# Earlier weight chunks, spread first sums and rearranged ends in a thresholded attention and squared-ReLU FFN kernel

## The chip, the core and the metric

The kernel runs on one core of a Trainium2 chip. The core has five engines that run side by side and wait for each other through semaphores: TensorE (PE; its weight loads are listed as PEld), VectorE (DVE), ScalarE (ACT), GpSimd (POOL) and SyncE (SP), which here only issues DMA transfers. Matrix products go to PSUM, everything else lies in SBUF, and large tensors lie in HBM. The metric is the device time of one execution in microseconds, from the first to the last instruction.

## What is computed

The reference, cut to what matters:

```python
# q, k, v: (8, 8, 576, 64) float32; tau = 0.02; w_in (512, 2048), w_out (2048, 512)
scores = q @ k.T / 8
scores = where(scores >= max(scores) - tau, scores, -1e9)
attn = exp(scores - max(scores)); attn = attn / (sum(attn) + 1e-9)
x = (attn @ v), as (4608, 512)           # batch and sequence x heads and head size
h = maximum(x @ w_in, 0.0)
out = (h * h) @ w_out                    # (4608, 512)
```

The two weight matrices arrive as float64, since their scaling in numpy made them so; the kernel turns them into float32 itself.

## The kernel before

**Attention.** Two heads make a pair, and there are 32 pairs (`pairs`, line 265). Each pair's 576 query rows are cut into five blocks (four of 128, one of 64 for both heads), so there are 160 blocks (`slots`, line 482). `slot(n)` (line 556) is an order written out by hand: in program order it names, for each engine, what is done for block n and its neighbours. Scores are computed three blocks ahead (`ahead(n + 3, ...)`), the softmax follows in steps (`stage`, `second`: maximum on DVE, exponential on ACT, threshold and sum on DVE, reciprocal on DVE at line 387, normalising on GpSimd at line 396), the weights are transposed on TensorE (line 437) and copied out of PSUM by ACT (line 439), and the product with v (line 467) gives a block of x^T, which is stored to HBM (`give_x`, `ask`). Score tiles (`sc`) have two PSUM buffers and so have all other PSUM tiles of this stage (`b`).

`load(i)` (line 268) asks for q and k of a pair: for each of the two, two transfers for the first 512 rows of both heads and one for the remaining 64 rows. All requests go out on the SP queue in program order, and a request whose buffer isn't free holds up those behind it. `turn(i)` transposes q and k, and `turn_last(i, ...)` does the remaining rows; after that the next pair is asked for.

**Weights.** Between these steps the weights are converted. There are 32 chunks of 512 KB as they arrive (16 of w_out, then 16 of w_in; `chunks`, line 161). `starts` (line 530) gives the block at which each begins: every second block from 0 for w_out, and every second block from `IN_FIRST` = 76 for w_in. With the chunk that begins at block s, `fetch` is called in block s - 1 and asks for it on the SP queue, into one of three buffers `raw`; `convert1` (ACT, line 201) and `convert2` (ACT) are in block s + 1, `convert3` (GpSimd) in s + 2, `convert4` and `convert5` (DVE) in s + 3, and `convert6` (GpSimd, line 239) in s + 4 makes the float32 chunk and frees the buffer.

**Sums.** The FFN multiplies 2x2 blocks of blocks with seven products in place of eight, on two levels, so that 49 products of sums are made. `sums` makes the sums of the weights on GpSimd, one per block by `sums_step`: those of w_out from block 35 on (`OUT_SUMS`, 44 of them), those of w_in from block 111 on (`IN_SUMS`). The first 512 tokens' sums of x^T (`prepare_x(0, ...)`, 12 of them) are made on GpSimd inside the attention: `load_x(0)` after block 24, and one sum after each block from 26 on (lines 885 to 889).

**FFN.** The tokens go through in nine steps of 512. `hidden_layer(n, also)` makes squared hidden values and stores them to HBM; when all steps are done, `output_layer(n, also)` makes the output. In each, a loop over seven outer products (`OUTER`) runs `inner`, with seven inner ones of four matmuls each; `inner` hands four finished quarters of an outer product to `final`. In the output layer, `final` adds into `t3` on DVE, and after `inner` one instruction on GpSimd (`sums_to(slice(1, 4), nc.gpsimd, ...)`, line 855) adds three of the four quarters to the running sums U2, U3 and to the output tile `o`. After the outer products 5 and 3, which end a half of the output rows, four stores are put in the list `later`; `ask()` issues them on the SP queue, at a later tick or, for the last half of the last step, after everything (line 983).

**The ends.** The program begins with building the identity matrix, asking for tau (line 110), `load(0)`, `load_v(0)`, the transposes of the first pair, and three blocks from -3 on that only start scores.

Of the kernel before, what the change touches and what calls it, by code (L numbers as in the profile page):

```python
# [11 lines left out]
I32 = mybir.dt.int32  # L12
# [36 lines left out]
def kernel(  # L49
# [25 lines left out]
    nc = tc.nc  # L75
    B, H, S, D = q.shape
    P = 128
# [8 lines left out]
    MAIN = FULL * P  # L86
    STEP = 512
    NSTEP = B * S // STEP
# [15 lines left out]
    sb = Region(arena, 0, X_AT[0])  # L104
# [2 lines left out]
    make_identity(nc, ident)  # L107

    tau_c = const.tile([P, 1], FP32, name="tau_c")
    nc.sync.dma_start(  # L110
        out=tau_c[:, :], in_=bass.AP(tensor=tau.tensor, offset=tau.offset, ap=[[0, P], [1, 1]])
    )

# [18 lines left out]
    def plus(e, out, x, y):  # L132
        e.tensor_tensor(out=out, in0=x, in1=y, op=ALU.add)  # L133
# [26 lines left out]
    WC = 512  # L160
# [11 lines left out]
    def fetch(m):  # L172
        if m is None:
            return
        src = chunks[m][3]
        three = (lambda t: t.rearrange("p (k o) -> p k o", k=4)) if m < 16 else (lambda t: t)
        if src.dtype == FP32:
            nc.sync.dma_start(out=three(weight(m)[:, :]), in_=src)
            return
        raw = sb.tile([P, 2 * WC], I32, tag="raw", bufs=3, name="raw")  # L180
        nc.sync.dma_start(out=three(raw[:, :]), in_=src.bitcast(I32))
        raws[m] = raw

# [78 lines left out]
    later = deque()  # L262
# [5 lines left out]
    def load(i):  # L268
        b, hp = pairs[i]
        h = 2 * hp  # L270
        qn = sb.tile([P, FULL, P], FP32, tag="qn", name="qn")
        kn = sb.tile([P, FULL, P], FP32, tag="kn", name="kn")

        rn = sb.tile([P, P], FP32, tag="rn", name="rn")

        for src, dst, order, rows in ((q, qn, "(t p) d -> p t d", 0), (k, kn, "(p t) d -> p t d", REST)):
            for j in range(2):
                nc.sync.dma_start(out=dst[:, :, ds(j * D, D)], in_=src[b, h + j, 0:MAIN, :].rearrange(order, p=P))
            nc.sync.dma_start(
                out=rn[ds(rows, REST), :].rearrange("p (j d) -> p j d", j=2),  # L280
                in_=src[b, h : h + 2, MAIN:S, :].rearrange("j p d -> p j d"),
            )
        loaded[i] = (qn, kn, rn)

    def load_v(i):
        b, hp = pairs[i]
        h = 2 * hp
        va = sb.tile([P, 2, FULL, D], FP32, tag="va", bufs=2, name="va")
        vd = vdiag[i % 2]
        nc.sync.dma_start(out=va[:, :, :, :], in_=v[b, h : h + 2, 0:MAIN, :].rearrange("j (p t) d -> p j t d", p=P))  # L290
        for j in range(2):
            nc.sync.dma_start(out=vd[ds(j * D, D), ds(j * D, D)], in_=v[b, h + j, MAIN:S, :])
        loaded_v[i] = (va, vd)

    def turn(i):

        qn, kn, rn = loaded.pop(i)
        qT = sb.tile([P, S], FP32, tag="qT", bufs=2, name="qT")
        kT = sb.tile([P, S], FP32, tag="kT", bufs=2, name="kT")
        turning[i] = (qT, kT, rn)  # L300
        for nat, to in ((qn, qT), (kn, kT)):
            pt = bank([P, FULL, P], "pqk")
            for t in range(FULL):
                nc.tensor.transpose(pt[:, t, :], nat[:, t, :], ident[:, :])
            flat, to = pt[:, :, :].rearrange("p t m -> p (t m)"), to[:, 0:MAIN]
            if nat is kn:
                nc.scalar.copy(to, flat)  # L307
            else:
                nc.scalar.activation(out=to, in_=flat, func=AF.Identity, scale=qscale[:, :])
            yield  # L310
# [242 lines left out]
    def begun(n):  # L553
        return starts.get(n)

    def slot(n):

        sums_start(n)
        ask()
        turn_part(n - 1, "w")  # L560
        convert4(begun(n - 3))
        convert3(begun(n - 2))
        stage(n + 2)
        turn_step(n, 0)
        values_and_load(n - 2)
        convert1(begun(n - 1))
        stage(n + 1)
        second(n + 1)
        turn_part(n - 1, "R")
        second(n + 2)  # L570
        sums_step()
        turn_part(n - 1, "W")
        convert6(begun(n - 4))
        stage(n + 2)
        second(n + 2)
        fetch(begun(n + 1))
        convert5(begun(n - 3))
        ahead(n + 3, 0)
        stage(n + 1)
        turn_step(n, 1)  # L580
        ahead(n + 3, 1)
        convert2(begun(n - 1))
# [229 lines left out]
    def output_layer(n, also):  # L812
        bank = lambda: banks.tile([P, BANK], FP32, tag="b", bufs=6, name="po")[:, 0:P]
        temp = lambda name: fin.tile([P, P], FP32, tag="t")
        AT = {(0, 0): 0, (1, 1): 1, (1, 0): 2, (0, 1): 3}
        U2 = fin.tile([P, 4, P], FP32, tag="u")
        U3 = fin.tile([P, 4, P], FP32, tag="u")
        o = {}
        for m in OUTER:
            where = {2: (0, 0), 4: (1, 0), 5: (1, 1), 3: (0, 1)}.get(m)  # L820
            if where and where[0] not in o:
                o[where[0]] = fin.tile([P, 2, 4, P], FP32, tag="o")
            mine = U3 if m in (4, 5) else U2
            t3 = fin.tile([P, 3, P], FP32, tag="t3") if m != 1 else None

            def product(to, k, more):
                g, w = operands[n, m, k], W_OUT[m, k].rearrange("p (k o) -> p k o", k=4)
                for j in range(4):
                    nc.tensor.matmul(  # L829
                        to, g[:, j, :], w[:, j, :], start=(not more and j == 0), stop=(j == 3), skip_group_check=True  # L830
                    )

            def sums_to(i, e, c):

                if where:
                    plus(e, o[where[0]][:, where[1], i, :], c, mine[:, i, :])
                if m in (5, 6):
                    plus(e, U2[:, i, :], c, U2[:, i, :])
                if m == 7:
                    plus(e, U3[:, i, :], c, U2[:, i, :])  # L840

            def final(ab, c, other):
                i = AT[ab]
                if m == 1 and other is None:
                    nc.scalar.copy(U2[:, i, :], c)
                elif m == 1:
                    plus(nc.vector, U2[:, i, :], c, other)
                elif other is None:
                    sums_to(i, nc.vector, c)
                else:  # L850
                    plus(nc.vector, t3[:, i - 1, :], c, other)

            inner(product, copy, temp, bank, final, lambda at: also(m, at))
            if m != 1:
                sums_to(slice(1, 4), nc.gpsimd, t3[:, :, :])
            if m in (5, 3):
                row = where[0]
                for (a, b), i in AT.items():
                    to = out[ds(n * STEP + row * 2 * NQ + a * NQ, NQ), :].rearrange("p (c b o) -> p c b o", c=2, b=2)
                    later.append((to[:, :, b, :], o[row][:, :, i, :]))  # L860


    def spread(work, at):
# [5 lines left out]
    with tc.manual_schedule():  # L869
        with ExitStack() as stack:  # L870
            sc_pool = stack.enter_context(tc.tile_pool(name="sc", bufs=2, space=PSUM))
            b_pool = stack.enter_context(tc.tile_pool(name="b", bufs=2, space=PSUM))

            def bank(shape, name):
                return b_pool.tile(shape, FP32, tag="b", name=name)

            load(0)
            load_v(0)
            for _ in turn(0):
                pass  # L880
            turn_last(0, bank([P, P], "pqkr")[:, :])()
            load_v(1)
            for n in range(-3, len(slots)):
                slot(n)
                if n == 24:
                    load_x(0)
                    xsums = prepare_x(0, lambda op, out, x, y: op(nc.gpsimd, out, x, y))
                if n > 25:
                    next(xsums, None)
            n = len(slots)  # L890

            def drain():

                while pending:
                    pt, m, of = pending.popleft()
                    xr = sb.tile([P, 2, P], FP32, tag="xr", bufs=3)
                    nc.scalar.copy(xr[:, 0, 0:m], pt[:, 0, 0:m])
                    give_x(of, xr)

            drain()  # L900
            values_and_load(n - 2)
            for part in "RWw":
                turn_part(n - 1, part)
            values_and_load(n - 1)
            drain()
            for _ in range(60):
                sums_step()
            ask()
# [111 lines left out]
```

## Time and profile before

| | |
|---|---|
| time, median of 3 | 1486.08 us (1485.96 to 1487.52) |
| span of the profiled execution | 1487.0 us, clock 0.994 |
| PE / DVE / ACT / POOL busy | 97% / 68% / 60% / 71% |
| attention, block 0 to its last copy (line 897) | 18.2 to 682.9 us |
| FFN, both layers | 682.9 to 1487.0 us |
| DMA, mean over the span | 119 GB/s |

A profile page gives for each engine its busy time, and the span in forty slices with the busy share of each in tenths. The list of waits says which engine sat idle in front of which line and what ended that: "ACT arena L201 <- DMA ..." is ScalarE idle before line 201 until a transfer landed. The chain of waits is followed back from the last instruction, and each of its pieces is the one that released the next. In the timeline a row has the start, the time, the engine, line and operation, and in brackets the idle time ahead of it. A row of busy time by stretch has the stretch, its length, the busy time of PE, PEld, DVE, ACT and POOL with the number of instructions, the granted TensorE clock, the busy share of the DMA engines and GB/s. An engine's mean busy share says little here, since the attention, the hidden layer and the output layer have different limits.

### The profile page before, as it was taken

The numbers are of one execution on the slowest core, as the hardware profiler recorded it, in microseconds if no ns is written. First come the engines' busy times: TensorE is split into PE (matmuls) and PEld (weight loads), VectorE is DVE, ScalarE is ACT, GpSimd is POOL, SyncE is SP. The second block draws the span as 40 slices with busy tenths as digits, with TensorE's granted clock in tenths as the row PEclk, the third lists the DMA queues.
The fourth block names the chain that finished last, engine by engine and source line by source line (L and its number), as shares of the span: only waits on it lengthen the run. The fifth ranks groups of instructions, "written<-read, shape, count | busy, mean of one in ns | idle before, by whom it ended". The sixth has DMA issues, their size and how long they took to land.

```text
span 1487.0 us, 35254 instructions
## 1 busy us (share of the span) xinstructions
PE 1437.3 (97%) x12880; PEld 1214.7 (82%) x12880; DVE 1006.9 (68%) x2149; ACT 888.9 (60%) x1792; POOL 1052.9 (71%) x1319
## 2 busy tenths in 40 slices
PE   6999999999999999999999999999999999999998
PEld 3665566665666666668999999999999999999998
DVE  4877766667777666775778877778755666555653
ACT  4887777767877777765666656767543333323330
POOL 3777987877767887773666555566677787777775
PEclk9999999999999999999999999999999999999999
DMA  4345223557343222212332334332994432244411
GB/s 110 104 118 156 61 54 97 166 175 218 100 117 106 64 63 56 58 40 67 121 126 95 114 114 143 135 122 100 368 333 143 143 111 82 98 139 143 143 29 29
DMA packets 212956, 176.90 MB, mean 119 GB/s; under 512 B 99888, under 2 KB 161328, under 8 KB 212784
## 3 DMA queue, kind: packets, MB, share of 16 engines
q1 hardware_dynamic: 212784, 174.65, 37.5%
q8 instruction: 102, 1.67, 0.5%
q14 instruction: 70, 0.57, 0.1%
HBM read 105.12 MB, written 69.47 MB: 117 GB/s over the span
## 4 chain that ended last, share of the span: by engine, by line
PE 61%; DVE 15%; ACT 8%; POOL 6%; DMA 5%; issue 3%; SPq 1%; POOLq 0%; DVEq 0%; ACTq 0%
PE po L829 27%; PE ph L706 21%; DVE arena L381 9%; ACT arena L376 5%; PE sc L353 5%; DVE arena L364 4%; PE pvR L467 3%; PE pwT L437 3%; PE sc L338 2%; POOL arena L396 1%; DVE arena L133 1%; DMA w<-w 1%; POOL w L130 1%; ACT arena L307 1%; POOL arena L133 1%
## 5 line engine op out<-in xcount | busy, mean ns | idle before, releaser
L133 POOL TENSOR_TENSOR arena<-arena 128x512 f32<-128x512 f32 (+1 forms) x315 | 377.5, 1221 | 258.5 <-DVE arena L133 220.7
L829 PE MATMUL po<-w,arena 128*128 128x128 f32 x3528 | 397.9, 276 | 2.1 <-ACT arena L620 1.8
L829 PEld LDWEIGHTS po<-w,arena 128*128 128x128 f32 x3528 | 396.3, 193 | 3.6 <-ACT arena L620 2.0
L706 PE MATMUL ph<-arena,w 128*128 128x128 f32 x3528 | 396.6, 275 | 2.1 <-DVE arena L133 1.1
L706 PEld LDWEIGHTS ph<-arena,w 128*128 128x128 f32 x3528 | 394.7, 192 | 3.9 <-DVE arena L133 3.5
L133 DVE TENSOR_TENSOR arena<-ph,arena 128x512 f32<-128x512 f32 x378 | 255.5, 688 | 93.9 <-PE ph L706 53.7
L364 DVE TENSOR_REDUCE arena<-sc 128x1 f32<-128x576 f32 x288 | 217.3, 755 | 131.6 <-PE sc L353 131.6
L381 DVE SCALAR_TENSOR_TENSOR arena<-sc,arena 128x576 f32<-128x576 f32 x288 | 224.5, 813 | 21.8 <-ACT arena L376 21.2
L396 POOL TENSOR_SCALAR arena<-arena 128x576 f32<-128x576 f32 (+1 forms) x320 | 223.0, 707 | 7.5 <-DVE arena L387 3.3
L133 DVE TENSOR_TENSOR arena<-po,arena 128x128 f32<-128x128 f32 x378 | 108.0, 289 | 172.1 <-PE po L829 169.2
L652 ACT COPY c<-arena 128x512 f32<-128x512 f32 (+1 forms) x303 | 172.7, 579 | 62.1 <-DVE arena L130 56.3
L376 ACT ACTIVATE arena<-sc,arena 128x576 f32<-128x576 f32 x288 | 200.7, 747 | 14.3 <-DVE arena L364 9.9
L437 PEld LDWEIGHTS pwT<-ident,arena 128*128 128x128 f32 x1152 | 128.6, 141 | 90.5 <-issue 36.2
L437 PE MATMUL pwT<-ident,arena 128*128 128x128 f32 x1152 | 181.5, 280 | 12.9 <-ACT arena L416 9.5
L353 PE MATMUL sc<-arena 64*128 64x512 f32 (+2 forms) x768 | 185.8, 575 | 1.3 <-DVE arena L381 1.0
L130 POOL TENSOR_TENSOR arena<-arena 128x512 f32<-128x512 f32 (+1 forms) x138 | 174.9, 1267 | 9.7
L130 DVE TENSOR_TENSOR arena<-arena,c 128x512 f32<-128x512 f32 (+1 forms) x267 | 174.5, 662 | 7.5 <-ACT c L652 6.9
L439 ACT COPY arena<-pwT 128x512 f32<-128x512 f32 x256 | 151.6, 592 | 46.1 <-PE pwT L437 36.3
L467 PE MATMUL pvR<-arena 128*64 128x128 f32 (+1 forms) x2560 | 164.2, 269 | 5.0 <-ACT arena L439 0.7
L467 PEld LDWEIGHTS pvR<-arena 128*64 128x64 f32 x2560 | 128.6, 137 | 34.9 <-issue 19.6
L685 ACT ACTIVATE arena<-arena 128x512 f32<-128x512 f32 x144 | 89.9, 624 | 77.6 <-POOL arena L133 77.6
L620 ACT COPY arena<-po 128x128 f32<-128x128 f32 x63 | 16.7, 265 | 180.5 <-PE po L829 178.5
(53 smaller groups left out, 1147.3 us busy)
## 6 DMA issues: line engine op xcount, KB each, us to landing
g<-arena SPq DMA_DIRECT2D x144, 256.0 KB, 2.0
arena<-g SPq DMA_DIRECT2D x144, 256.0 KB, 4.6
w<-w SPq DMA_DIRECT2D x98, 256.0 KB, 4.8
out_dram<-arena SPq DMA_DIRECT2D x72, 128.0 KB, 2.2
arena<-in_q_dram SPq DMA_DIRECT2D x64, 128.0 KB, 2.7
arena<-in_k_dram SPq DMA_DIRECT2D x64, 128.0 KB, 2.9
arena<-in_v_dram SPq DMA_DIRECT2D x32, 256.0 KB, 2.8
arena<-in_moe_w_out_dram SPq DMA_DIRECT2D x16, 512.0 KB, 4.2
```

The costliest lines, as they stand in the source:

```text
L130: e.tensor_tensor(out=out, in0=x, in1=y, op=ALU.subtract)
L133: e.tensor_tensor(out=out, in0=x, in1=y, op=ALU.add)
L353: nc.tensor.matmul(to, qT[rows, ds(t * P, m)], kT[rows, ds(k0, n)], start=True, stop=True)
L364: nc.vector.tensor_reduce(out=nmx[:, j : j + 1], in_=sc[:, ds(at[j], S)], axis=AXIS.X, op=ALU.max, negate=True)
L376: nc.scalar.activation(out=w[:, ts(j, S)], in_=sc[:, ds(at[j], S)], func=AF.Exp, bias=nmx[:, j : j + 1], scale=1.0)
L381: nc.vector.scalar_tensor_tensor(out=w[:, ts(j, S)], in0=sc[:, ds(at[j], S)], scalar=thr[:, j : j + 1], in1=w[:, ts(j, S)], op0=ALU.is_ge, ...
L396: nc.gpsimd.tensor_scalar(out=out, in0=w, scalar1=r, scalar2=1.0, op0=ALU.mult, op1=ALU.mult)
L437: nc.tensor.transpose(pt[:, c, :], w[:, ds(j * (S + REST) + c * P, P)], ident[:, :])
L467: nc.tensor.matmul(pv[rows, :], va[:, j, c, :], wT[:, j, c, 0:n], start=(c == 0), stop=False, skip_group_check=True)
L652: nc.scalar.copy(c, y)
L706: nc.tensor.matmul(to[:, j, :], W_IN[m, k][:, ts(j, P)], of[k][:, m - 1, :], start=(not more and j == 0), stop=True, skip_group_check=True,)
L829: nc.tensor.matmul(to, g[:, j, :], w[:, j, :], start=(not more and j == 0), stop=(j == 3), skip_group_check=True)
```

## The change

It has four parts. Weight chunks are asked for two blocks sooner, and four raw buffers take the place of three. The load and the sums of the first x^T are moved from blocks 24 to 37 to blocks 76 to 111, and one sum is made every third block instead of every block. At the start, tau and the first pair's k are asked for on the ACT queue instead of the SP queue, so that two sequencers issue at once, and TensorE gets transposes of the identity that nobody reads (ten at first, twelve after each of blocks -2 and -1), which are meant to bring its clock up. At the end, the last outer product of the last step makes its last sums on DVE, quarter by quarter, and stores each at once, in turn on the SP and the ACT queue, instead of one sum on GpSimd and stores after it.

```diff
-    nc.sync.dma_start(
+    nc.scalar.dma_start(
         out=tau_c[:, :], in_=bass.AP(tensor=tau.tensor, offset=tau.offset, ap=[[0, P], [1, 1]])
...
-        raw = sb.tile([P, 2 * WC], I32, tag="raw", bufs=3, name="raw")
+        raw = sb.tile([P, 2 * WC], I32, tag="raw", bufs=4, name="raw")
...
+            queue = nc.scalar if i == 0 and src is k else nc.sync
             for j in range(2):
-                nc.sync.dma_start(out=dst[:, :, ds(j * D, D)], in_=src[b, h + j, 0:MAIN, :].rearrange(order, p=P))
-            nc.sync.dma_start(
+                queue.dma_start(out=dst[:, :, ds(j * D, D)], in_=src[b, h + j, 0:MAIN, :].rearrange(order, p=P))
+            queue.dma_start(
...
-        fetch(begun(n + 1))
+        fetch(begun(n + 3))
...
+        def give_out(row, ab, queue):
+            a, b = ab
+            to = out[ds(n * STEP + row * 2 * NQ + a * NQ, NQ), :].rearrange("p (c b o) -> p c b o", c=2, b=2)
+            if queue is None:
+                later.append((to[:, :, b, :], o[row][:, :, AT[ab], :]))
+            else:
+                queue.dma_start(out=to[:, :, b, :], in_=o[row][:, :, AT[ab], :])
...
+            at_end = n == NSTEP - 1 and m == OUTER[-1]
...
                 else:
                     plus(nc.vector, t3[:, i - 1, :], c, other)
+                    if at_end:
+                        sums_to(i, nc.vector, t3[:, i - 1, :])
+                if at_end:
+                    give_out(0, ab, nc.sync if i % 2 else nc.scalar)
...
-            if m != 1:
+            if m != 1 and not at_end:
                 sums_to(slice(1, 4), nc.gpsimd, t3[:, :, :])
...
+            def keep_busy(times):
+                pt = bank([P, P], "idle")
+                for _ in range(times):
+                    nc.tensor.transpose(pt[:, :], ident[:, :], ident[:, :])
...
+            keep_busy(10)
             for _ in turn(0):
                 pass
...
                 slot(n)
-                if n == 24:
+                if -3 < n < 0:
+                    keep_busy(12)
+                if n == IN_FIRST:
                     load_x(0)
                     xsums = prepare_x(0, lambda op, out, x, y: op(nc.gpsimd, out, x, y))
-                if n > 25:
+                if n > IN_FIRST + 1 and n % 3 == 0:
                     next(xsums, None)
```

More of the change, by code (lines that the diff above doesn't have):

```diff
@@ L851, in final @@
                     plus(nc.vector, t3[:, i - 1, :], c, other)
+                    if at_end:
+                        sums_to(i, nc.vector, t3[:, i - 1, :])
+                if at_end:
+                    give_out(0, ab, nc.sync if i % 2 else nc.scalar)
             inner(product, copy, temp, bank, final, lambda at: also(m, at))
-            if m != 1:
+            if m != 1 and not at_end:
                 sums_to(slice(1, 4), nc.gpsimd, t3[:, :, :])
[L856 to L860, printed above, removed]
+            if m in (5, 3) and not at_end:
+                for ab in AT:
+                    give_out(where[0], ab, None)
     def spread(work, at):
```

## The prediction

> **What bounds the kernel now.** I read the page first, then the waits, then the chain and the timeline of single stretches, then busy time by stretch, since one share over 1487 us mixes three stages. The page:
>
> ```profile
> PE 1437.3 (97%) x12880; PEld 1214.7 (82%) x12880; DVE 1006.9 (68%) x2149; ACT 888.9 (60%) x1792; POOL 1052.9 (71%) x1319
> PE   6999999999999999999999999999999999999998
> ```
>
> TensorE is busy everywhere but in the first slice. So time can come only from places where the matmul stream is held up, and the FFN (from 683 us, PE idle under 4 us until the end by the gaps between its matmuls in the trace) is nearly full. I therefore took the starts of the 160 reciprocals of line 387, one per attention block, and summed them by tens. Ten blocks take 40.0 us where no chunk is converted (482 to 642 us), 42.4 us where chunks of w_out are converted (60.8 to 103.1), 44.8 and 43.2 us where the first sums of x^T run (103.1 to 191.1), and 43.8, 44.0 and 42.7 us where w_in is converted (351.8 to 482.4). So 40.0 is the floor that TensorE sets, and the excess has to be explained. The waits:
>
> ```profile
> ACT arena L201 <- DMA arena<-in_moe_w_in_dram: 12.4, 4, 4.0
> ACT arena L201 <- DMA arena<-in_moe_w_out_dram: 5.9, 2, 2.9
> ```
>
> The columns are total us, number and longest us. ACT waits for a chunk six times, 18.3 us in all. The chain around one of them (start, us, what):
>
> ```profile
> 408.21 0.63 SPq L279
> 408.84 0.05 issue
> 408.89 0.03 SPq L181
> 408.92 0.03 issue
> 408.95 4.66 DMA arena<-in_moe_w_in_dram
> 413.61 0.02 issue
> 413.63 0.02 ACT arena L201
> ```
>
> The chunk's request stands in the SP queue behind six requests for the next q and k (403.7 to 408.8), is issued 4.66 us before it lands, and `convert1` starts 0.02 us after the landing. Five of the six waits have this shape: they follow blocks 11 and 21 for w_out and 81, 91 and 101 for w_in, where both kinds of request fall in one block. The sixth (block 79) is a late chunk behind the stores of finished sums. For the x^T sums, busy time by stretch (PE, PEld, DVE, ACT, POOL):
>
> ```profile
> 60.80:103.10 42.30, 39.83 (x366) 26.26 (x364) 32.97 (x75) 34.24 (x73) 31.26 (x55) 1.00 0.45 119
> 147.90:165.00 17.10, 14.53 (x141) 9.75 (x139) 13.32 (x28) 12.51 (x28) 16.07 (x25) 1.00 0.30 75
> 230.80:271.00 40.20, 39.40 (x366) 26.30 (x368) 27.66 (x66) 28.89 (x63) 32.33 (x54) 1.00 0.37 106
> ```
>
> With one x^T sum per block and a conversion per two blocks GpSimd is busy 16.07 of 17.10 us: there it is the bound, and nowhere else. Last, both ends; the timeline of TensorE at the start, and of the last output:
>
> ```profile
> 4.46 1.09 PE L304 MATMUL pqk<-ident,arena 128*128 128x128 f32 x4 [4.46 <-DMA arena<-in_q_dram]
> 7.02 1.09 PE L304 MATMUL pqk<-ident,arena 128*128 128x128 f32 x4 [1.47 <-DMA arena<-in_k_dram]
> 10.50 2.08 PE L353 MATMUL sc<-arena 64*128 64x512 f32 x4
> 23.56 2.08 PE L353 MATMUL sc<-arena 64*128 64x512 f32 x4
> ...
> 1481.15 0.29 DVE L133 TENSOR_TENSOR arena<-po,arena 128x128 f32<-128x128 f32 x1 [0.60 <-PE po L829]
> 1481.58 0.99 POOL L133 TENSOR_TENSOR arena<-arena 128x384 f32<-128x384 f32 x1 [4.36 <-DVE arena L133]
> ```
>
> Four score matmuls take 2.08 us here and 1.13 at 32.3 us; four transposes 1.09 against 0.66 at 25.6: the first 25 us run on a slow clock, and between 0 and 18.2 us TensorE is idle 9.8 us. At the end the last sum on GpSimd ends 1.1 us after the last product's sum, three stores are issued after it at 1482.60, 1483.18 and 1483.85, the last lands at 1486.03, and the program ends 1.0 us later.
>
> **What the Trainium skill says.** "TensorE: Matmul & The Clock Gate", Part 1: the array runs at half clock until a free-running window of some 3.4 us was busy, and falls back after an idle one. The trace agrees: the granted clock changes at multiples of 3.41 us, and the cold pitch of transposes is 0.21 us against 0.11 warm. It also shows a cold window at 414.7 us, right after the wait quoted above. The same page, "Architectural detail": ACT, VectorE and GpSimd take their instructions in strict order; so behind a waiting `convert1` stands the block's copy of transposed weights (line 439), and TensorE waits for that. "DMA: Bandwidth & Descriptors", "Issuing engines are not separate DMA queues": a second issuing engine saves only issue time. That is what the change wants at the start, where SP spends 0.4 to 0.76 us on each of seven requests.
>
> **The change part by part.**
>
> *Chunks two blocks sooner, four buffers.* No instruction is added. A request for chunk m goes out two blocks (8 us) earlier and needs the buffer of chunk m-4, whose `convert6` is one block ahead of it, just as the buffer of m-3 was one block ahead before: SP's own wait doesn't grow, and queued behind it stand, as before, the stores of x^T and the q and k loads. The longest wait is 4.04 us, under 8 us of new slack, so all six should go. Worth: the interval 4 to 5, the same place in the pattern with a chunk that was in time, took 4.02 us. The waits' intervals took 5.93, 5.94, 6.73, 7.02 and 6.24, and the intervals that follow are otherwise the same (4.48, 3.89), so none of it is caught up. w_out: 1.91 + 1.92 = 3.8. For w_in I take whole tens, since the cold window and the sixth wait are in there: ten converting blocks without a wait are 42.4 - 1.9 = 40.5; 43.8 + 44.0 + 42.7 - 3 x 40.5 = 9.0, and 0.3 in the ten before. Sum 13.1.
>
> *x^T sums to blocks 78 to 111, one in three.* Removed from blocks 26 to 37: the ten from 103.1 lose 44.78 - 42.40 = 2.38, those from 147.9 lose 43.15 - 40.2 = 2.95 (half of them convert), less 0.23 by which the next ten (39.77) ran short: 5.1. Added: 12 sums of 1.25 us on GpSimd while w_in is converted. There it is busy 31.3 of 40.5 us in ten blocks; 3.3 sums make it 35.4, so on average they lie in idle time. But every second one falls into a block with `convert3` (0.67) and `convert6` (1.04), and behind it queue the threshold, the 1e-9 sum and the normalising, for which DVE and then TensorE wait. Bounds: 0, if backlog vanishes in the next block, and 12 x 1.5 = 18 (1.25 and the 0.24 us of gaps per block that the bound stretch shows). GpSimd has a mean 0.9 us idle per block there; I take 0.25 each, 3.0. The load of 1 MB for it moves along and is hidden at both places.
>
> *Start.* k on the ACT queue: its second request goes out at about 1.7 instead of 3.62 us; both pairs share 193 GB/s (busy time by stretch, 3 to 4 us), 0.58 MB in 3.0 us from 2.2, so k is there at about 5.2 to 5.4 instead of 6.89: 1.5. tau on ACT costs 0.4 of issue and keeps its landing near 3.3. The ten dummy transposes (10 x 0.21) end by about 3.9, before q lands at 4.3. Twice twelve more lie in TensorE's waits for DVE (2.42 us at 15.3, 1.37 at 20.6) and cost nothing if warm (1.3), a few tenths if cold (2.6). If the clock stays up, the second scores are done 1.1 sooner (DVE waits 1.31 for them), the third 0.3, the fourth 1.5. Where the window falls is open; of these 2.9, and up to 1.0 for the first scores, I take 2.6. Sum 4.1, bounds 1.3 to 5.5.
>
> *End.* Each sum of the last product is made on DVE (a 128x128 one takes 0.29) and stored at once on two queues. After the last: 1481.44 + 0.29, issue, landing 2.12 later: 1483.88 against 1486.03: 2.15. The three earlier pairs fit in the 0.60 us of DVE's idle time between products.
>
> Total: 13.1 + 5.1 - 3.0 + 4.1 + 2.2 = 21.5; 1486.1 - 21.5 = 1464.6.
>
> **The rivals.** *GpSimd becomes the bound while w_in is converted:* the twelve sums cost 1.5 each. For it: normalising already releases TensorE there (short PEld waits for line 396). Against: the 0.9 us of idle time per block. 1464.6 - 3.0 + 18 = 1479.6. *Chunks stay late,* held by buffers that come back late: SP waits for line 239 seven times, up to 2.2 us. Against: the same one block of slack. Without the 13.1: 1477.7. *All goes well:* the sums are free and the clock is warm from the first scores: 1464.6 - 3.0 - 1.4 = 1460.2. *Slower:* earlier requests block the SP queue, ahead of x^T's stores, whose three buffers ACT needs, and 1 us is lost at each of 32 chunks, with no wait removed: 1477.7 + 32 = 1509.7. Against: SP waits for ACT in every block anyway.
>
> **How the numbers follow.** Forecast 0.66, GpSimd bound 0.14, late chunks 0.08, all well 0.08, slower 0.04. The range takes in the all-well case with its small errors (1458) and goes up half-way into the first rivals (1475). Faster: all but the last and a sliver for gains that cancel: 0.94; same 0.02; slower 0.04.
>
> **What would show it.** No ACT wait at line 201 for a chunk; tens of blocks near 40.5 in both converting stretches, 40.0 in blocks 35 to 45; the cold window at 414.7 gone; GpSimd at about 35.5 us in ten w_in blocks, and no PE wait on line 396 that grew; k's transposes at about 5.5 us; the last store landing 2.7 us after the last matmul. Wrong would be tens near 42 with GpSimd waits in blocks 78 to 111, or SP waits at line 181 that grew beyond a block.

## Result, and the profile after

The changed kernel takes 1465.42 us (median, 1464.52 to 1466.85) against 1486.53 us of the kernel before beside it: a ratio of 0.9858, 95% interval 0.9841 to 0.9875. It is faster by 21.1 us; 1464.6 us was forecast. The total was right; its parts were less so, and the experiments show which.

The page of the changed kernel, the same two lines as before:

```profile
PE 1435.4 (98%) x12914; PEld 1216.6 (83%) x12914; DVE 1006.8 (69%) x2152; ACT 889.1 (61%) x1792; POOL 1050.9 (72%) x1318
PE   7999999999999999999999999999999999999998
```

The engines do the same work; the span around it is 22.1 us shorter (1464.9 against 1487.0). In the list of waits no ACT wait at line 201 is left. In its place stands a new one, 3.6 us in all (engine, line, what ended it: total us, times, longest):

```profile
ACT arena L418 <- DMA xT<-arena: 3.6, 2, 2.9
```

The reciprocals, one per block, say where the time went. The table has the time of ten blocks each, from the starts in the traces (in us; "sums undone" is an experiment below):

| blocks | before | after | chunks alone | sums undone |
|---|---|---|---|---|
| start to block 0 | 18.2 | 17.6 | 17.7 | 18.1 |
| 0 to 9 | 42.58 | 40.49 | 43.22 | 40.48 |
| 10 to 19 | 42.39 | 39.98 | 39.99 | 39.99 |
| 20 to 29 | 44.78 | 39.98 | 42.36 | 42.39 |
| 30 to 39 | 43.15 | 39.40 | 43.10 | 43.08 |
| 40 to 49 | 39.77 | 39.98 | 39.77 | 39.77 |
| 70 to 79 | 40.59 | 43.29 | 40.60 | 40.59 |
| 80 to 89 | 43.83 | 41.05 | 40.05 | 39.99 |
| 90 to 99 | 44.02 | 40.24 | 40.00 | 39.99 |
| 100 to 109 | 42.70 | 40.24 | 39.99 | 40.05 |
| last output matmul to the end | 5.93 | 3.95 | 5.94 | 3.93 |

From the first reciprocal to the last it is 657.3 us before and 637.5 after, and the two FFN layers take 798.2 and 798.1. So 19.8 us lie in the attention and 2.0 behind the last matmul. The 0.6 us ahead of block 0 can't be told from chance: the first reciprocal comes at 17.6 to 18.4 us in the seven profiles whose start is written as in the changed kernel, and at 17.7 and 18.2 in the two with the old start. Blocks 0 to 9 also differ between these two, 43.22 and 42.58, though their start is the same: the slow clock lasted until 28.1 us in one and 25.6 in the other. One row clearly went the wrong way: blocks 70 to 79 lost 2.7 us.

At both ends, the timelines of TensorE, and of the last output, of the changed kernel:

```profile
1.44 2.40 PE L897 MATMUL idle<-ident 128*128 128x128 f32 x10 [1.44 <-POOL ident masks.py:199]
4.65 1.09 PE L306 MATMUL pqk<-ident,arena 128*128 128x128 f32 x4 [0.81 <-DMA arena<-in_q_dram]
6.83 1.09 PE L306 MATMUL pqk<-ident,arena 128*128 128x128 f32 x4 [1.09 <-DMA arena<-in_k_dram]
10.30 2.08 PE L355 MATMUL sc<-arena 64*128 64x512 f32 x4
...
21.85 1.13 PE L355 MATMUL sc<-arena 64*128 64x512 f32 x4
...
1460.98 0.29 DVE L133 TENSOR_TENSOR arena<-po,arena 128x128 f32<-128x128 f32 x1 [0.27 <-PE po L843]
1461.31 0.29 DVE L133 TENSOR_TENSOR arena<-arena 128x128 f32<-128x128 f32 x1
```

The transposes of k start at 6.83 us, hardly sooner than before (7.02). The first scores (line 355) still run on the slow clock; the fourth block's (21.85, before 23.56) take 1.13 instead of 2.08 us. At the end the last sum is on DVE, and it ends 0.66 us after the last matmul.

### The profile page after: what moved, and what is told of

Its sections match the earlier page's. It is cut to its first block, busy times and chain, and to the rows that moved or that the text cites. A ratio compares the mean times of both kernels' runs of the same rounds, so it can differ in the third digit from the quotient of the medians.

```text
span 1464.9 us, 35324 instructions
## 1 busy us (share of the span) xinstructions
PE 1435.4 (98%) x12914; PEld 1216.6 (83%) x12914; DVE 1006.8 (69%) x2152; ACT 889.1 (61%) x1792; POOL 1050.9 (72%) x1318
```

## The experiments

All ratios are to runs of the kernel before on the same chip; its median was 1486.5 to 1489.0 us from chip to chip, so ratios are compared, not times. Their intervals are about 0.0015 to each side. Differences of one or two microseconds are read from stage times in the profiles.

**The chunks alone.** The kernel before, with

```diff
-        raw = sb.tile([P, 2 * WC], I32, tag="raw", bufs=3, name="raw")
+        raw = sb.tile([P, 2 * WC], I32, tag="raw", bufs=4, name="raw")
-        fetch(begun(n + 1))
+        fetch(begun(n + 3))
```

> The kernel before with only the four buffers and the requests two blocks sooner. Theory A (the prediction's: only the six waits at line 201 go, 13.1 us): 1473.4 us, and ten blocks that convert w_out (blocks 10 to 19) at 40.5 us. Theory B (a late chunk also disturbs the blocks around it, so that the whole excess over 40.0 goes, as the changed kernel's tens of 40.0 suggest): about 1469, blocks 10 to 19 at 40.0. Both: no ACT wait for a chunk, and the ten blocks with x^T sums (20 to 29) still over 42, since GpSimd is the bound there.

1472.39 us, ratio 0.9889 (0.9875 to 0.9904): 16.3 us, by far the most of the gain. Theory A's 13.1 us would be a ratio of 0.991, outside the interval; theory B's 1469 us would be 0.988, inside it. The wait for chunks is gone. The view of line 201 of the kernel before, with what ended ACT's idle time ahead of it:

```profile
L201 ACT ACTIVATE arena<-arena x32: 653/700/739, 26.8 to 472.1; 128x512 f32<-128x512 f32 x32
  DMA arena<-in_moe_w_in_dram: 12.4, 4
  DMA arena<-in_moe_w_out_dram: 5.9, 2
```

and with the chunks alone, where no line of waits follows:

```profile
L201 ACT ACTIVATE arena<-arena x32: 681/704/745, 27.2 to 456.8; 128x512 f32<-128x512 f32 x32
```

(The three numbers are the shortest, median and longest duration in ns.) Blocks 10 to 19 take 39.99 us, so theory B's sum holds (its reason doesn't, see below): ten blocks that convert five chunks take as long as ten that convert none. Busy time of that stretch (PE, PEld, DVE, ACT, POOL, then clock, DMA share, GB/s) beside the one shown of before:

```profile
60.90:100.90 40.00, 39.57 (x366) 26.22 (x364) 33.05 (x75) 34.57 (x73) 31.38 (x55) 1.00 0.45 126
```

The same work, DMA share too, in 40.00 instead of 42.30 us: TensorE is full and DVE, ACT and GpSimd carry the conversion beside it. The interval of a late chunk, 5.93 us, became 3.53: a late chunk cost 2.40 us, not 1.91. Blocks 20 to 39 stayed at 42.4 and 43.1, as expected of the x^T sums.

**The chunks undone** in the changed kernel.

```diff
-        raw = sb.tile([P, 2 * WC], I32, tag="raw", bufs=4, name="raw")
+        raw = sb.tile([P, 2 * WC], I32, tag="raw", bufs=3, name="raw")
-        fetch(begun(n + 3))
+        fetch(begun(n + 1))
```

> The changed kernel with three buffers and the requests one block ahead again. Theory A: the six waits come back, +13.1: 1478.5. Theory B: +17: 1482, tens of w_out at 42.4 again. If the other three parts had made the gain, it would stay at 1466.

1481.61 us, ratio 0.9954 (0.9939 to 0.9969). The waits are back (the list of waits):

```profile
ACT arena L201 <- DMA arena<-in_moe_w_in_dram: 12.5, 4, 4.2
ACT arena L201 <- DMA arena<-in_moe_w_out_dram: 7.8, 2, 4.0
```

and blocks 10 to 19 take 43.41 us. From the first reciprocal to the last it is 652.5 us, 15.0 more than in the changed kernel. (The spans differ by 13.6 only, since the changed kernel's profile has a slow clock in the output layer that costs it 1.6 us and this one hasn't; see the last section.) The ratios differ by 0.0096, or 14 us. So both ways the chunks are worth 14 to 16 us, and the other three parts together some 7. Between the two theories this run doesn't decide: 0.9946 and 0.997 would have been their ratios.

**One block sooner.** Three buffers again, and

```diff
-        fetch(begun(n + 3))
+        fetch(begun(n + 2))
```

> The changed kernel with the requests one block sooner than before instead of two, in three buffers; the buffer then comes free only in the block of the request. Theory (only the slack counts): the smallest slack between landing and first conversion, 3.0 us in the changed kernel, becomes about -1.0 at one or two chunks, so +1 to +2: 1467. Rival (SP is held behind the conversion in the same block, with x^T's stores and the q and k requests behind it): several waits come back, +5 to +10: 1473.

1466.31 us, ratio 0.9854 (0.9838 to 0.9871): the same as with two blocks and a fourth buffer. The rival's cause was there and did no harm: the SP queue waits much more at line 181 (SP's own waits),

```profile
SPq L181 <- POOL w L239: 53.3, 13, 5.5
SPq L181 <- POOL arena L398: 18.1, 5, 3.8
SPq L181 <- DVE arena L231: 7.3, 9, 1.6
```

80 us with a smaller group, against 24 us before and 20 in the changed kernel, and the blocks keep their 40.0 us. Only one chunk comes late, at block 79, by 0.04 us. The theory was nearly right on the time but not on the slack, which it put at -1.0. Five other chunks are again asked for straight behind the six requests for q and k, and they landed 0.8 to 1.6 us ahead of their conversion. That is what the waits of the kernel before lead one to expect: five of them, behind the same six requests, lasted 2.9 to 4.0 us, and a block is 4 us. So one block is enough here, but with little to spare.

**The x^T sums undone** in the changed kernel.

```diff
-                if n == IN_FIRST:
+                if n == 24:
...
-                if n > IN_FIRST + 1 and n % 3 == 0:
+                if n > 25:
```

> The changed kernel with the load and the sums of x^T at blocks 24 to 37, one per block, again. Theory: blocks 20 to 39 lose 5 us (GpSimd the bound), blocks 70 to 109 gain what they now cost over 40.0, 3.5 us of it a stall at block 80 that the load of 1 MB makes: net +0 to +2: 1466 to 1468. Rival: the stall at block 80 comes from the earlier chunk requests and the stores of finished sums, so it stays: +5: 1470.5.

1467.60 us, ratio 0.9858 (0.9843 to 0.9872): the same as the changed kernel. The table shows two amounts that nearly cancel: the move saves 5.9 us in blocks 20 to 49 (125.2 against 119.4) and costs 4.0 in blocks 70 to 119 (200.3 against 204.3). With the sums back, block 79 is followed by an interval of 4.30 instead of 6.98 us, so the stall there comes from what was moved there, not from the earlier chunks.

**The load alone put elsewhere, then load and sums.** In the changed kernel, first

```diff
-                if n == IN_FIRST:
+                if n == 40:
                     load_x(0)
```

> The changed kernel with the load of x^T (1 MB) after block 40 instead of 76, its sums left at 78 to 111. Theory (the load's 1 MB on the transfer engines makes the interval of 6.98 us after block 79): that interval goes to 4.3, blocks 70 to 79 take 40.6 instead of 43.3, and the time falls by about 2.7: ratio to the kernel before 0.984 (1463 where before is 1487). Rival (the first sums of x^T on GpSimd beside the last sums of w_out make it): the interval stays, ratio 0.986.

1463.63 us, ratio 0.9831 (0.9816 to 0.9846). Blocks 70 to 89 take 82.1 instead of 84.3 us, and the wait for a store of x^T is gone. So 2.2 of the 4.0 us were the 1 MB load. (In the five profiles that have this part as in the changed kernel, blocks 70 to 89 take 83.1 to 84.5 us, so the load cost 1.0 to 2.4 us; the ratios of the two kernels overlap.) What it did is seen in the changed kernel's timeline of the SP queue (start, us, line, number) and of ACT:

```profile
332.12 2.12 SPq L641 DMA_DIRECT2D arena<-xT  x4
334.64 0.33 SPq L547 DMA_DIRECT2D xT<-arena  x1
335.07 0.38 SPq L181 DMA_DIRECT2D arena<-in_moe_w_in_dram  x1
335.56 0.85 SPq L547 DMA_DIRECT2D xT<-arena  x2
336.50 0.40 SPq L181 DMA_DIRECT2D arena<-in_moe_w_in_dram  x1
...
339.27 0.37 ACT L418 COPY arena<-pvR 128x256 f32<-128x256 f32 x1 [2.94 <-DMA xT<-arena]
```

Four loads of 256 KB, then two chunks of 512 KB and three small stores, all inside 4.8 us; the transfer engines are busy from 334 to 342 us (share 1.02 and 0.98; 0.88 and 0.99 with the load at block 40, so the sum of the traffic alone tells little). The waits of 325 to 345 us name two paths from there to the stall:

```profile
DVE arena L389 <- POOL arena L387: 4.3, 3, 2.6
ACT arena L418 <- DMA xT<-arena: 2.9, 1, 2.9
POOL arena L130 <- DMA arena<-xT: 2.3, 1, 2.3
PE pqk L306 <- ACT arena L418: 1.3, 1, 1.3
```

ACT may not write one of its three buffers `xr` again before the store from it has landed. The store at 334.64, 32 KB and behind the four loads, landed after 4.6 us (such stores take 2.1 in the kernel before), ACT went on at 339.27, and TensorE waited for ACT. The two stores of 64 KB behind it took 5.6 us (median) in place of 1.5. At the same time GpSimd stood at the first sum of x^T (line 130) until the load itself had landed, at 339.0 us, and behind that sum stood the step (line 387) that the next reciprocal waits for. With the load at block 40 both waits are gone, and the store behind the same block's k took 2.3 us. Which of the two made the stall longer no run separates.

Then load and sums from block 40 on:

```diff
-                if n == IN_FIRST:
+                if n == 40:
...
-                if n > IN_FIRST + 1 and n % 3 == 0:
+                if n > 41 and n % 3 == 0:
```

> The changed kernel with load and sums of x^T from block 40 on, one sum every third block to 75. There GpSimd has 32.3 of 40 us busy from the sums of w_out, and 3.3 sums of 1.25 make it 36.5. Theory (GpSimd has room, nothing else is in the way): these tens stay at 40.0 and the 4.2 us by which blocks 70 to 109 exceed the run with the sums undone go: ratio 0.983 (1461.5). Rival (a second sum in a block makes GpSimd late by up to 1.25 us in each of 12 blocks): tens at 41 to 43 and no gain.

1461.61 us, ratio 0.9819 (0.9804 to 0.9835). Blocks 80 to 109 take 40.00, 39.99 and 40.04 us, and blocks 40 to 59 take 80.0 as before. GpSimd was fuller there than before, while the time did not change:

```profile
183.00:223.00 40.00, 39.40 (x366) 26.22 (x364) 27.76 (x64) 28.96 (x63) 36.05 (x58) 1.00 0.25 61
```

36.05 of 40.00 us (fifth engine), against 32.33 of 40.20 in the stretch shown of before. This version beats both kernels: its interval lies below the changed kernel's (0.9841 to 0.9875).

**v later.** The first pair's v is asked for after its q and k are transposed:

```diff
             load(0)
-            load_v(0)
             keep_busy(10)
...
             turn_last(0, bank([P, P], "pqkr")[:, :])()
+            load_v(0)
             load_v(1)
```

> The changed kernel with the first pair's v asked for after the transposes of its q and k. In the changed kernel k's second half was asked for at 1.90 us and landed at 6.69, beside v's. Theory (the transfers share the engines, so v's go at the expense of k's): k lands at 5.3 to 5.6, the first scores start 1.2 us sooner, ratio 0.985. Rival (k is held by its own small packets): landing near 6.7, no change, 0.986.

1464.90 us, ratio 0.9839 (0.9821 to 0.9857), within the interval of the changed kernel. In its timeline k's transposes start 0.92 us sooner,

```profile
5.91 1.09 PE L306 MATMUL pqk<-ident,arena 128*128 128x128 f32 x4 [0.20 <-DMA arena<-in_k_dram]
```

since k's second half landed at 5.77 us instead of 6.69, but the first reciprocal comes only 0.5 us sooner (17.1): the scores behind it fell on the slow clock (12.12 us, 2.08 us for the second block, which took 1.13 in the changed kernel). Joined with load and sums from block 40:

> The load and sums of x^T from block 40 on and v later, together. If both theories hold the gains add: 4.2 + 1.2 under the changed kernel, ratio 0.982 (1460.5 where before is 1487). If either falls, that one's part is missing.

1461.37 us, ratio 0.9818 (0.9801 to 0.9834), not to be told from the version without it.

**k on the SP queue**, and tau with it.

```diff
-    nc.scalar.dma_start(
+    nc.sync.dma_start(
         out=tau_c[:, :], in_=bass.AP(tensor=tau.tensor, offset=tau.offset, ap=[[0, P], [1, 1]])
...
-            queue = nc.scalar if i == 0 and src is k else nc.sync
+            queue = nc.sync
```

> The changed kernel with tau and the first k asked for on the SP queue again. The changed kernel's k landed at 6.69 us, the one before's at 6.89. Theory (the shared transfer engines and v's requests took back what the second queue saved): the first block's reciprocal at 17.4 to 18.2 instead of 17.6, time within 0.6 of the changed kernel. Rival (the prediction's): +1.5.

1466.13 us, ratio 0.9850 (0.9835 to 0.9866). k's second half landed at 6.59 us on the SP queue and at 6.69 on its own; first reciprocal at 17.9 and 17.6. Over all profiles k lands at 6.6 to 6.9 us from the SP queue (three) and at 6.2 to 7.2 from its own beside v (eight), so no worth of the second queue is shown as long as v is asked for beside it. With v later, k lands at 5.8 to 6.1 (three). A piece that was not foreseen: the end took 4.52 us instead of 3.95, since the last store, on SP, landed after 2.70 instead of 2.12 us. Why is open.

**No dummy transposes.**

```diff
-            keep_busy(10)
...
-                if -3 < n < 0:
-                    keep_busy(12)
```

> The changed kernel without the dummy transposes (10, 12 and 12). Theory (the clock falls back at about 19 us as it did before, so that the scores of the fourth block are slow again, 2.08 instead of 1.13 us for four matmuls, and the transposes beside them 1.1 instead of 0.6): the reciprocals of blocks 0 to 10 take 42.6 us instead of 40.5, time +2 to +2.5 over the changed kernel, ratio 0.987. Rival (the dummies do nothing that the work itself does not do): no change, 0.985.

1469.47 us, ratio 0.9871 (0.9855 to 0.9887). Blocks 0 to 9 take 43.78 instead of 40.49 us, with the first reciprocal 0.2 us sooner: the dummies are worth 3.1 us in the profile (2 by the ratios). They keep the clock up through blocks 2 to 4, as TensorE without them shows:

```profile
17.00 0.77 PE L340 MATMUL sc<-arena 128*128 128x128 f32 x2 [2.42 <-DVE arena L383]
17.70 2.08 PE L355 MATMUL sc<-arena 64*128 64x512 f32 x4
19.71 1.12 PE L306 MATMUL pqk<-ident,arena 128*128 128x128 f32 x4
22.20 0.77 PE L340 MATMUL sc<-arena 128*128 128x128 f32 x2 [1.37 <-DVE arena L383]
```

Four scores take 2.08 us instead of 1.13 still at 17.7 us. The idle times of 2.42 and 1.37 us are those in which the changed kernel runs its twelve dummies.

**Eight more dummies**, between the first transposes and the first scores, on top of the joined version:

```diff
             turn_last(0, bank([P, P], "pqkr")[:, :])()
+            keep_busy(8)
             load_v(0)
```

> x^T from block 40 on, v later, and eight more dummy transposes between the first pair's transposes and the first scores. Theory (the clock of the first two blocks' scores is the start's next limit): the first four score matmuls take 1.13 instead of 2.08 us, and the first reciprocal comes 1 us sooner: 16.0 to 16.5, ratio 0.981. Rival (where the clock's window falls decides, eight more are not enough or come too late): first scores at 2.08, no change from the joined kernel, 0.982.

1461.47 us, ratio 0.9819 (0.9804 to 0.9835): the first scores stay at 2.08 us,

```profile
8.01 1.97 PE L897 MATMUL idle<-ident 128*128 128x128 f32 x8 [0.46 <-ACT arena L309]
10.33 2.08 PE L355 MATMUL sc<-arena 64*128 64x512 f32 x4
```

the rival's case.

**The end undone.**

```diff
-            at_end = n == NSTEP - 1 and m == OUTER[-1]
+            at_end = False
```

> The changed kernel with the old end: one sum on GpSimd, then the stores on one queue. Theory: from the last output matmul to the end 5.93 us instead of 3.95, time +2.0, all else alike.

1467.26 us, ratio 0.9859 (0.9839 to 0.9879). From the last output matmul to the end 5.95 instead of 3.95 us: 2.0, as expected. By ratio alone this would not be seen.

## Why the prediction was right, and where it was not

- **Chunks, 13.1 us forecast.** The mechanism was right: the six waits go, and each was in its own interval. The size was too small: 15.3 us by the tens of the chunks alone (2.40 and 2.42 in blocks 10 to 29, 3.78, 4.02 and 2.71 in blocks 80 to 109; the 0.3 taken for blocks 70 to 79 did not show). The term that was mis-sized is the interval without a wait. I took 4.02 us from blocks 4 to 5, which lie in the start; in the settled pattern it is 3.53. From that came "ten converting blocks without a wait are 40.5"; they are 40.0. Of theory B only the sum holds: with w_out nothing around the late chunk changed but its own interval. (With w_in one following interval did, 5.06 us beside 4.48, where the clock was slow.)
- **x^T sums, 5.1 saved and 3.0 paid.** 5.9 and 4.0 by the runs; net 1.9 against 2.1. The first is more in blocks 30 to 39, which take 39.40 us without the sums where I took 40.2: the wrong 40.5 explains 0.25 of that, the rest is a ten that is itself shorter than 40.0. The second has another cause than forecast for about half of it: "the load of 1 MB moves along and is hidden at both places" is the step that failed. 2.2 us came from that load, by the two waits shown above. The twelve sums on GpSimd cost 1.8, 0.15 each in the mean where I took 0.25, but not evenly: 1.5 lies in the intervals of blocks 79 to 82, where the first two sums fall, and 0.3 in all that follow. The rival with GpSimd as the bound (1.5 each) is out.
- **Start, 4.1.** 2.1 by the profiles, in blocks 0 to 9 (2.7 against the chunks alone, which has the old start too); the 0.6 up to block 0 is within what equal starts differ by. k's 1.5 us failed: I let q and k share the engines and forgot that a shorter SP queue brings v's requests forward as well, at 2.56 instead of 4.97 us. The second queue did what the prediction cites from the Trainium skill ("DMA: Bandwidth & Descriptors", "Issuing engines are not separate DMA queues"), it saved issue time (k's second request went out at 1.90 instead of 3.62 us), but k landed no sooner until v was asked for later. The dummies' 2.6 was near: 3.1 with and without them, 2.1 against the kernel before, whose clock came up by itself at 25.6 us. What the prediction takes from "TensorE: Matmul & The Clock Gate" of the Trainium skill, Part 1, that the clock falls back after an idle window, does not fit this trace: the windows ahead of a fall were not idle (last section).
- **End, 2.15.** 2.0.
- **Rivals.** Chunks that stay late, and a blocked SP queue that costs time, are out: with one block of lead SP waited three times as long at the chunk requests, and nothing was lost.

The errors, +2.2, -0.2, -2.0 and -0.2, nearly cancel, so it is luck in part that the forecast saving came within half a microsecond of the measured one. The forecast's 21.5 is 21.3 by these terms, 22.1 by the profiles and 21.1 by the medians; of the 0.8 us between terms and profiles 0.6 lie ahead of block 0, and the rest is not explained.

## What to carry to other kernels

Where a load is late only in some blocks, look at what else stands in the issuing queue there; one block of lead was just enough here, and the longer waits of the queue cost nothing. Take the time of an undisturbed interval from the settled part of a run, and test it by its neighbours: mine came from the start and was 0.5 us off, once in every ten blocks. A load that "moves along" is not free: before it is moved, add up what the transfer engines carry in the new place, who needs it how soon, and which small store with few buffers is behind it. Before a microsecond of the start is credited to an edit, compare profiles that share the same start: here they differed by 0.8 us.

## What the runs showed of the hardware

Stores of 64 KB, 1.5 us in the median of the kernel before, took 5.6 us among 2 MB of loads. The second half of the first k, 128 KB in packets of 256 bytes, landed at 6.6 to 6.9 us from one queue, 3.0 to 3.3 us after its request; from a second queue at 6.2 to 7.2 beside v and at 5.8 to 6.1 without it, 3.9 to 5.3 us after its request. Eighteen dummy transposes ahead of the first scores left these on the slow clock in the profile taken, while twelve after each of blocks -2 and -1 kept it up in every profile that had them. It took no idle window to bring the clock down: in the kernel before TensorE was busy for 1.05 us of the 3.41 us ahead of the slow stretch at 18.8 us, 0.87 of 3.42 ahead of the one at 414.7 and 1.60 of 3.42 ahead of the one at 1087.2. A share like the last did not always do it: in the run with the load at block 40 TensorE was busy for 1.59 of 3.41 us at the same place (1061.3), and the clock stayed up. And the output layer took 400.0 us in the profiles of the kernels before and after and of two experiments, but 398.4 in the other ten: there the slow-clock window of 3.4 us at its beginning (1067.8 us in the changed kernel) was missing. A comparison of single profiles has to leave 1.6 us for that.
